# Attention by whole head-pair blocks instead of two-tile units, in a scheduled kernel of banded attention and two MLPs

## The chip, the cores and the metric

The kernel runs on one core of a Trainium2 chip. The metric is the device time of one execution in microseconds (us). A change counts as measured here when it moves the time by more than about 0.5%, 4.8 us.

## What is computed

Cut to what matters, with B, H, S, D = 4, 8, 576, 64, 512 model columns and 2048 hidden columns:

```python
scores = scale * np.matmul(q, k.transpose(0, 1, 3, 2))
mask = (rel >= 0) & (rel < 128)                     # each row sees itself and 127 rows before
scores = np.where(mask, scores + bias[None], -1e9)  # bias: a slope per head times -|rel|
attn = np.exp(scores - np.max(scores, axis=-1, keepdims=True))
attn = attn / (np.sum(attn, axis=-1, keepdims=True) + 1e-09)
x = np.matmul(attn, v)                              # laid out as 2304 rows x 512
h = x @ w_in                                        # first MLP, rational activation
g = (a0 + a1*h + a2*h*h + a3*h*h*h) / (1 + |b0|*|h| + |b1|*h*h + 1e-6)
x2 = g @ w_out
h2 = x2 @ w2_in                                     # second MLP, SiLU
out = (h2 / (1 + np.exp(-h2))) @ w2_out
```

## The kernel before, in words

The 2304 rows are 18 tiles of 128. The first MLP works on five blocks of 4, 4, 3, 4 and 3 tiles (`blk1`), the second on five of 4, 4, 4, 3 and 3 (`blk2`). A block takes 16 steps, one for each 128 of the 2048 hidden columns. A step makes h for its columns with 12 products (L726 to L728: four slices of the 512 model columns, each as high part by high part, high by low and low by high, since every fp32 operand is split into two fp32r halves), runs the activation on it and, two steps later (`lag`), adds 12 products into the block's accumulators (L805 to L807, in the second MLP L843 to L845). The first two blocks run interleaved (ten steps of block 0, ten of block 1, then six and six); then come blocks 2, 3, 4, and the second MLP's blocks 5 to 9.

The activation of the first MLP is six ScalarE (ACT) and six VectorE (DVE) instructions in a chain (L743 to L772). The last, `t3<-t1,h` at L772, frees the PSUM buffer of h; there are two of those (`hb`), so PE's h products wait for L772 of two steps before. Then g is split: `gh` is a cast of t3 (by ACT, DVE or POOL, as `OPT['gh']` allows), `gl` the remainder t3 - gh (POOL or DVE, `OPT['gl']`).

Weights are loaded as 64-bit numbers and put together by three instructions, one on ACT (L480) and two on DVE (`raw_w`, `raw_wo`: L482 and L484), then split into a high part (`hi`, L389 or L397) and a low part (`lo`, a TENSOR_TENSOR at L404 on DVE or L408 on POOL). For the second MLP `OPT['w2lo']` says who makes the low part. These 32 weights are prepared during block 4 and at the start of block 5.

Attention of a block runs ahead of its MLP steps, one head pair after another (four in a block). Before the change its unit is two tiles of one head pair (`unit`, 40 units). A unit has scores for both heads (`s`, L571), the other band half put in by a predicated copy (L580), mask and row maximum (L589), exp with row sums (L593), 1/sum (`l`, L604 and L605), normalization of `e` (L609 on POOL or L614 on ACT), transposes (`pt`, L625), the two masked halves (`ph`, L632 and L637), products with v (`av`, L662), a copy of `av` out of PSUM (`xr`, L389), and, once a head pair's block is complete, the split of `xr` into `xh` and `xl`, the operands of h.

The order on every engine is not written by hand. `plan_kernel` lists operations with a priority (in units of steps), one or several engines with a cost each, and what they read and write; `schedule` then simulates the engines with these costs, takes in turn the operation of least priority number among those that could start soonest (`look`, in ns), and chooses the engine. The instructions are issued in that order, and each engine executes its own queue strictly in order. The constants of `OPT` with decimals (`dS`, `dT`, `dA`: scores, transposes and products with v; `x2p`: loads of the second MLP's input; `pw`, `pwo`: weights; `wpro`, `lead`: pace of attention) are shifts of these priorities. `spin` products on an identity matrix fill PE's planned pauses before the first h.

Of the kernel before, what the change touches and what calls it, by code (L numbers as in the profile page):

```python
# [312 lines left out]
def plan_kernel(ctx, tc, qn, kn, vp, table, w1, wo1, a4, b2, w2, wo2, out):  # L313
# [231 lines left out]
    def unit(u, pS, pT, pA, w):  # L545
        gi, tiles = units[u]
        bi, hp = groups[gi]
        i0 = tiles[0] - blk_start[bi]
# [29 lines left out]
        if two:  # L578
            for hh in range(2):
                pl.op(pS + (0.05 + 0.01 * hh) * w, "dve", c_dve(nt_ * P), lambda hh=hh: nc.vector.copy_predicated(  # L580
                    T[S_[hh]][:, two, c1], tab[:, 4:5].bitcast(U32).broadcast_to([P, nt_, P]), T[S_[hh]][:, two, 0:P]),
                    reads=[("tab", 0)], writes=[S_[hh]])

        def mx(ti, hh):
            if ti == 0 and hh == 0:
                T[E_] = e_p.tile([P, 2, 2, P], F32, tag="e", name=f"e{u}")
                T[M_] = st_p.tile([P, 2, 2], F32, tag="m", name=f"m{u}")
                T[L_] = st_p.tile([P, 4, 1], F32, tag="l", name=f"l{u}")
            nc.vector.tensor_tensor_reduce(out=T[E_][:, ti, hh], in0=T[S_[hh]][:, ti, c1], in1=tabs[:, 2 * hp + hh, TABLE.get(tiles[ti], 0)],  # L589
                                           scale=-0.125, scalar=3.0e38, op0=ALU.add, op1=ALU.min, accum_out=T[M_][:, ti, hh:hh + 1])  # L590
# [30 lines left out]
        def tr():  # L621
            T[PT] = bank(PTT).tile([P, 2, 2, P], F32, tag=PTT, name=f"pt{u}")
            for ti in range(m):
                for hh in range(2):
                    nc.tensor.transpose(T[PT][:, ti, hh], T[E_][:, ti, hh], ident)  # L625
# [413 lines left out]
```

## Time and profile before

| what | value |
|---|---|
| median of 3 runs | 961.26 us (960.0 to 964.73) |
| profiled execution | 960.95 us, span of its instructions 959.2 us |
| PE (matmul) busy | 923.7 us, 96% of the span |
| DVE busy | 534.1 us, 56% |
| ACT busy | 550.9 us, 57% |
| POOL busy | 297.6 us, 31% |
| PE waits put down to DVE at L772 | 22.2 us in 26 waits |

The share of an engine over the whole span says little here, since the first 556 us (attention and first MLP) and the rest (second MLP) have different limits. The profile is therefore read by stretches. "fp32" matmuls appear as two records each, and matmul records overlap, so PE's pace is read from start to start.

### The profile page before, as it was taken

The numbers are of one execution on the slowest core, as the hardware profiler recorded it, in microseconds if no ns is written. First come the engines' busy times: TensorE is split into PE (matmuls) and PEld (weight loads), VectorE is DVE, ScalarE is ACT, GpSimd is POOL, SyncE is SP. The second block draws the span as 40 slices with busy tenths as digits, with TensorE's granted clock in tenths as the row PEclk, the third lists the DMA queues.
The fourth block names the chain that finished last, engine by engine and source line by source line (L and its number), as shares of the span: only waits on it lengthen the run. The fifth ranks groups of instructions, "written<-read, shape, count | busy, mean of one in ns | idle before, by whom it ended". The sixth has DMA issues, their size and how long they took to land.

```text
span 959.2 us, 13416 instructions
## 1 busy us (share of the span) xinstructions
PE 923.7 (96%) x4712; PEld 764.5 (80%) x4712; DVE 534.1 (56%) x1237; ACT 550.9 (57%) x1185; POOL 297.6 (31%) x277
## 2 busy tenths in 40 slices
PE   8879899999999999999988899999999999999998
PEld 6656677876678888777888888888888888999997
DVE  5889998789889888888899887200001000000000
ACT  6989898897676776766788675232223222222222
POOL 1134543454222122223222463342223223222221
PEclk9989999999999999999999999999999999999999
DMA  8365773476655334322475576111002000100000
GB/s 262 121 202 184 230 255 125 150 223 227 202 173 170 126 118 138 113 66 88 139 234 181 172 223 215 34 34 44 1 1 77 1 1 1 45 1 1 33 1 33
DMA packets 53842, 111.36 MB, mean 116 GB/s; under 512 B 4752, under 2 KB 24208, under 8 KB 53776
## 3 DMA queue, kind: packets, MB, share of 16 engines
q1 hardware_dynamic: 53776, 110.51, 35.7%
q8 instruction: 37, 0.61, 0.3%
q14 instruction: 29, 0.24, 0.1%
HBM read 90.57 MB, written 19.92 MB: 115 GB/s over the span
## 4 chain that ended last, share of the span: by engine, by line
PE 75%; DVE 11%; ACT 6%; DMA 5%; issue 2%; SPq 0%; POOL 0%; ACTq 0%; POOLq 0%; DVEq 0%
PE h L726 13%; PE h L728 12%; PE h L727 12%; PE acc L845 7%; PE acc L844 7%; PE acc L843 7%; PE acc L805 4%; PE acc L807 4%; PE acc L806 4%; PE s L571 3%; PE av L662 2%; DVE t L757 2%; DMA raw_wo<-in_wo 2%; ACT t L749 1%; DVE t L772 1%
## 5 line engine op out<-in xcount | busy, mean ns | idle before, releaser
L408 POOL TENSOR_TENSOR gl<-t,gh 128x512 fp32r<-128x512 f32 (+1 forms) x151 | 183.8, 1217 | 471.8 <-ACT gh L389 338.4
L779 ACT ACTIVATE t<-h 128x512 f32<-128x512 f32 (+1 forms) x80 | 44.5, 556 | 243.7 <-PE h L728 243.3
L805 PE MATMUL acc<-gh,wo 128*128 128x512 f32 (+1 forms) x320 | 123.3, 385 | 1.4 <-DVE x L826 0.8
L807 PE MATMUL acc<-gl,wo 128*128 128x512 f32 (+1 forms) x320 | 118.4, 370 | 0.0
L726 PE MATMUL h<-x2h,w 128*128 128x512 f32 (+1 forms) x320 | 118.0, 369 | 0.4 <-DVE t L772 0.4
L806 PE MATMUL acc<-gh,wo 128*128 128x512 f32 (+1 forms) x320 | 118.0, 369 | 0.0
L728 PE MATMUL h<-x2h,w 128*128 128x512 f32 (+1 forms) x320 | 117.9, 368 | 0.0
L727 PE MATMUL h<-x2l,w 128*128 128x512 f32 (+1 forms) x320 | 117.7, 368 | 0.0
L845 PE MATMUL acc<-wo,gl 128*128 128x512 f32 x288 | 112.7, 391 | 0.0
L844 PE MATMUL acc<-wo,gh 128*128 128x512 f32 x288 | 112.6, 391 | 0.0
L843 PE MATMUL acc<-wo,gh 128*128 128x512 f32 x288 | 112.0, 389 | 0.0
L726 PE MATMUL h<-xh,ws 128*128 128x512 f32 (+1 forms) x256 | 97.3, 380 | 11.6 <-DVE t L772 11.4
L404 DVE TENSOR_TENSOR x2l<-x2r,x2h 128x512 fp32r<-128x512 f32 (+1 forms) x8 | 7.0, 892 | 179.5 <-ACT x2h L389 179.5
L728 PE MATMUL h<-xh,ws 128*128 128x512 f32 (+1 forms) x256 | 93.6, 366 | 0.0
L727 PE MATMUL h<-xl,ws 128*128 128x512 f32 (+1 forms) x256 | 93.5, 365 | 0.0
L389 ACT CAST gh<-t 128x512 fp32r<-128x512 f32 (+1 forms) x141 | 81.1, 576 | 18.7 <-DVE t L772 15.4
L805 PEld LDWEIGHTS acc<-gh,wo 128*128 128x128 f32 x320 | 60.3, 188 | 16.3 <-issue 6.9
L726 PEld LDWEIGHTS h<-xh,ws 128*128 128x128 f32 x256 | 48.3, 189 | 25.9 <-DVE t L772 18.7
L726 PEld LDWEIGHTS h<-x2h,w 128*128 128x128 f32 x320 | 60.1, 188 | 9.8 <-PE acc L807 0.7
L743 ACT ACTIVATE t<-h,ab 128x512 f32<-128x512 f32 (+1 forms) x80 | 51.3, 641 | 28.5 <-PE h L728 28.2
L727 PEld LDWEIGHTS h<-x2l,w 128*128 128x128 f32 x320 | 60.1, 188 | 8.8
L807 PEld LDWEIGHTS acc<-gl,wo 128*128 128x128 f32 x320 | 60.2, 188 | 8.5 <-POOL gl L408 0.5
(86 smaller groups left out, 1850.0 us busy)
## 6 DMA issues: line engine op xcount, KB each, us to landing
ws<-sc SPq DMA_DIRECT2D x64, 512.0 KB, 3.3
raw_w<-in_w SPq DMA_DIRECT2D x32, 512.0 KB, 4.5
raw_wo<-in_wo SPq DMA_DIRECT2D x32, 512.0 KB, 4.5
sc<-w SPq DMA_DIRECT2D x16, 512.0 KB, 4.9
out<-out SPq DMA_DIRECT2D x18, 256.0 KB, 2.0
kd<-in_kn SPq DMA_DIRECT2D x12, 256.0 KB, 3.6
qd<-in_qn SPq DMA_DIRECT2D x12, 256.0 KB, 4.1
vh<-in_vp SPq DMA_DIRECT2D x12, 256.0 KB, 4.2
```

Of the source, the lines that this page charges most:

```text
L389: nc.scalar.activation(out=o, in_=i, func=AF.Copy, scale=sc) if scale is not None else nc.scalar.copy(o, i)
L408: nc.gpsimd.tensor_tensor(out=o, in0=a, in1=b, op=op)
L726: nc.tensor.matmul(o, lhsT=T[W][:, 0, c], rhs=xh, start=kt == 0, stop=False)
L727: nc.tensor.matmul(o, lhsT=T[W][:, 0, c], rhs=xl, start=False, stop=False)
L728: nc.tensor.matmul(o, lhsT=T[W][:, 1, c], rhs=xh, start=False, stop=kt == KD - 1)
L743: nc.scalar.activation(out=t("t2"), in_=hp_(), func=AF.Abs, scale=ab[:, 1:2])
L805: nc.tensor.matmul(a, lhsT=T[WO][:, 0, c], rhs=T[G1][:, :n], start=first_f, stop=False)
L806: nc.tensor.matmul(a, lhsT=T[WO][:, 1, c], rhs=T[G1][:, :n], start=False, stop=False)
L807: nc.tensor.matmul(a, lhsT=T[WO][:, 0, c], rhs=T[G2][:, :n], start=False, stop=last_f)
L843: nc.tensor.matmul(T[A], lhsT=T[G1][:, c], rhs=T[WO][:, 0], start=f == 0, stop=False)
L844: nc.tensor.matmul(T[A], lhsT=T[G1][:, c], rhs=T[WO][:, 1], start=False, stop=False)
L845: nc.tensor.matmul(T[A], lhsT=T[G2][:, c], rhs=T[WO][:, 0], start=False, stop=f == KF - 1)
```

## The change

The unit of attention becomes a head pair's whole block of 3 or 4 tiles (`group`, 20 groups). Scores, predicated copies, maxima and exps still run in halves of two tiles; the 1/sum is one pair of instructions for the group; normalization and transposes run in halves into two PSUM banks, one for each head; the masked halves are made for each head over the whole block; the products with v are one accumulation over up to 512 columns; and `xh` and `xl` are made straight from that PSUM bank, without `xr`. The allowed engines change (`gl` and the weights' low parts only on POOL, `gh` also on POOL, evacuations only on ACT), buffers of `e` and `ph` go from 3 and 2 to 2 and 1 (of larger tiles), and the priority shifts get other values.

```diff
-    'xh2': 'pool|act|dve',
-    'xl2': 'dve',
-    'gh': 'act|dve',
-    'gl': 'pool|dve',
+    'gh': 'act|dve|pool',
+    'gl': 'pool',
-    'evac': 'act|dve',
+    'evac': 'act',
-    'w2lo': 'dve',
-    'gl2': 'pool|dve',
+    'w2lo': 'pool',
+    'gl2': 'pool',
-    'eb': 3,
-    'ptb': 2,
+    'eb': 2,
+    'ptb': 1,
-    'tabs': 'pool|act',
+    'tabs': 'pool',
-    'wpro': 1.368,
-    'dS': -1,
+    'wpro': 1.204,
+    'dS': -1.576,
-    'dA': 0.194,
-    'dm': 0.315,
-    'look': 47.996,
-    'pw': -0.776,
-    'pwo': -1.143,
-    'x2p': 0.086,
+    'dA': 0.106,
+    'dm': 0.284,
+    'look': 28.673,
+    'pw': -0.74,
+    'pwo': -0.969,
+    'x2p': 1.653,
-    'dg': 0.371,
-    'lead': 2.2,
+    'dg': 0.44,
+    'lead': 2.526,
-    'gh0': 'act|pool',
+    'gh0': 'act',
...
-    def unit(u, pS, pT, pA, w):
-        gi, tiles = units[u]
+    def group(gi, pS, pT, pA, w):
         bi, hp = groups[gi]
+        t0, n = blk_start[bi], BLK1[bi]
+        tiles = list(range(t0, t0 + n))
...
+        ST = ("acc0", "acc1") if bi == 0 and gi % 2 else ("atA", "atB")
+        PTT = ("acc2", "acc3") if bi == 0 else ("atA", "atB")
+        AVT = ST[0] if bi == 0 else "atA"
+        halves = [range(a, min(a + 2, n)) for a in range(0, n, 2)]
...
+        ls = lambda a=0, b=n: T[L_][:, 2 * a:2 * b]
+        pl.op(pS + 0.5 * w, "dve", 100, lambda: nc.vector.tensor_scalar(out=ls(), in0=ls(), scalar1=1e-9, scalar2=None, op0=ALU.add), reads=[L_], writes=[L_])
+        pl.op(pS + 0.505 * w, "dve", 120, lambda: nc.vector.reciprocal(ls(), ls()), reads=[L_], writes=[L_])
...
+                nc.vector.tensor_tensor(out=T[PH][:, hh, :n, 0], in0=T[PT[hh]][:, :n], in1=own_mask().broadcast_to([P, n, P]), op=ALU.mult)
...
-            pl.op(pA + 0.1 * w, do_copy(OPT["xhi"], m * P, xraw, psum=True), 0, None, reads=[AV], writes=[XR + (i0,)])
...
+        pl.op(pA + 0.1 * w, do_copy(OPT["xhi"], n * P, xh_all, psum=True), 0, None, reads=[AV], writes=[XH, XL + ("a",)])
+        pl.op(pA + 0.15 * w, "dve", c_dve(n * P), lambda: nc.vector.tensor_tensor(
+            out=T[XL][:, :n * P], in0=T[AV][:, :n * P], in1=T[XH][:, :n * P].bitcast(F32), op=ALU.subtract), reads=[AV, XH], writes=[XL])
```

Where instructions moved, at the places that the prediction speaks of. First DVE in block 4, around steps 70 and 71 (in `t1_70`, `h70` the number is the step's; `raw_w25` is second-MLP weight 5, `wo22` an output weight 2). Before:

```order
L757 SCALAR_TENSOR_TENSOR t1_70_5492<-t2_70_5484,ab_113,h70_5454 128x384
L770 SCALAR_TENSOR_TENSOR h69_5405<-t3_69_5440,na_112,h69_5405 128x384
L761 TENSOR_TENSOR t3_70_5490<-t3_70_5490,h70_5454 128x384
L772 SCALAR_TENSOR_TENSOR t3_69_5440<-t1_69_5445,h69_5405 128x384
L762 SCALAR_TENSOR_TENSOR t3_70_5490<-t3_70_5490,na_112,h70_5454 128x384
L393 CAST gh69_5514<-t3_69_5440 128x384
L484 SCALAR_TENSOR_TENSOR raw_wo22_5338<-raw_wo22_5338 128x512
L768 SCALAR_TENSOR_TENSOR t1_70_5492<-t1_70_5492,h70_5454 128x384
L770 SCALAR_TENSOR_TENSOR h70_5454<-t3_70_5490,na_112,h70_5454 128x384
L404 TENSOR_TENSOR wo22_5527<-raw_wo22_5338,wo22_5527 128x512
L772 SCALAR_TENSOR_TENSOR t3_70_5490<-t1_70_5492,h70_5454 128x384
```

With the change:

```order
L760 SCALAR_TENSOR_TENSOR t1_70_5266<-t2_70_5253,ab_113,h70_5221 128x384
L775 SCALAR_TENSOR_TENSOR t3_69_5205<-t1_69_5211,h69_5171 128x384
L764 TENSOR_TENSOR t3_70_5258<-t3_70_5258,h70_5221 128x384
L482 SCALAR_TENSOR_TENSOR raw_w25_5158<-raw_w25_5158 128x512
L765 SCALAR_TENSOR_TENSOR t3_70_5258<-t3_70_5258,na_112,h70_5221 128x384
L480 TENSOR_SCALAR raw_wo23_5218<-raw_wo23_5218 128x512
L771 SCALAR_TENSOR_TENSOR t1_70_5266<-t1_70_5266,h70_5221 128x384
L773 SCALAR_TENSOR_TENSOR h70_5221<-t3_70_5258,na_112,h70_5221 128x384
L760 SCALAR_TENSOR_TENSOR t1_71_5320<-t2_71_5306,ab_113,h71_5275 128x384
L775 SCALAR_TENSOR_TENSOR t3_70_5258<-t1_70_5266,h70_5221 128x384
```

The low part (`wo22`) and the cast `gh69` are gone from DVE's queue; the six chain instructions of a step and the two that put a weight together stay.

POOL over the same steps, before:

```order
L408 TENSOR_TENSOR gl69_5524<-t3_69_5440,gh69_5514 128x384
L408 TENSOR_TENSOR gl70_5558<-t3_70_5490,gh70_5551 128x384
L408 TENSOR_TENSOR gl71_5620<-t3_71_5538,gh71_5616 128x384
L408 TENSOR_TENSOR gl72_5675<-t3_72_5592,gh72_5671 128x384
L408 TENSOR_TENSOR gl73_5725<-t3_73_5647,gh73_5714 128x384
```

With the change:

```order
L406 TENSOR_TENSOR gl69_5286<-t3_69_5205,gh69_5282 128x384
L406 TENSOR_TENSOR w25_5295<-raw_w25_5158,w25_5295 128x512
L395 TENSOR_SCALAR gh70_5335<-t3_70_5258 128x384
L406 TENSOR_TENSOR gl70_5339<-t3_70_5258,gh70_5335 128x384
L406 TENSOR_TENSOR wo23_5348<-raw_wo23_5218,wo23_5348 128x512
L395 TENSOR_SCALAR gh71_5388<-t3_71_5311 128x384
L406 TENSOR_TENSOR gl71_5392<-t3_71_5311,gh71_5388 128x384
```

In place of one instruction a step POOL now has three: the cast, the remainder, and a weight's low part.

Last, PE where the second MLP begins (`h80` is its first step, `acc4` the last accumulation of the first MLP). Before, from the second slice of h80 on:

```order
L728 MATMUL h80_5989<-x2h0_1_5810,w20_5100 128x512
L726 MATMUL h80_5989<-x2h0_2_5869,w20_5100 128x512
L727 MATMUL h80_5989<-x2l0_2_5876,w20_5100 128x512
L728 MATMUL h80_5989<-x2h0_2_5869,w20_5100 128x512
L726 MATMUL h80_5989<-x2h0_3_5905,w20_5100 128x512
L727 MATMUL h80_5989<-x2l0_3_5917,w20_5100 128x512
L728 MATMUL h80_5989<-x2h0_3_5905,w20_5100 128x512
L805 MATMUL acc4_0_0_5268<-gh78_5996,wo114_2439 128x384
```

With the change:

```order
L731 MATMUL h80_5764<-x2h0_1_5663,w20_4819 128x512
L808 MATMUL acc4_0_0_5036<-gh78_5756,wo114_2371 128x384
L809 MATMUL acc4_0_0_5036<-gh78_5756,wo114_2371 128x384
L810 MATMUL acc4_0_0_5036<-gl78_5771,wo114_2371 128x384
L808 MATMUL acc4_0_1_5044<-gh78_5756,wo114_2371 128x384
L809 MATMUL acc4_0_1_5044<-gh78_5756,wo114_2371 128x384
L810 MATMUL acc4_0_1_5044<-gl78_5771,wo114_2371 128x384
L808 MATMUL acc4_0_2_5052<-gh78_5756,wo114_2371 128x384
L809 MATMUL acc4_0_2_5052<-gh78_5756,wo114_2371 128x384
L810 MATMUL acc4_0_2_5052<-gl78_5771,wo114_2371 128x384
L729 MATMUL h80_5764<-x2h0_2_5758,w20_4819 128x512
L730 MATMUL h80_5764<-x2l0_2_5777,w20_4819 128x512
```

Before, all 12 products of h80 stood ahead of `acc4` for step 78; now the second half of h80 stands behind nine of those twelve. The third and fourth slices of the second MLP's input (`x2h0_2`, `x2h0_3`) are loaded later than before (`x2p`), and the products that need them moved back with them.

## Rows read from the trace of the kernel before

**Rows 1.** The page's first lines: span, busy time of each engine.
```profile
span 959.2 us, 13416 instructions
PE 923.7 (96%) x4712; PEld 764.5 (80%) x4712; DVE 534.1 (56%) x1237; ACT 550.9 (57%) x1185; POOL 297.6 (31%) x277
```
**Rows 2.** Who waited for whom: total us, times, longest; PE's first, DVE's table.
```profile
PE h L726 <- DVE t L772: 22.2, 26, 3.6
...
DVE s L580 <- DMA tab<-in_table: 7.0, 1, 7.0
```
**Rows 3.** Busy time by stretch: length, PE, PEld, DVE, ACT, POOL, clock, DMA, GB/s.
```profile
46.00:72.00 26.00, 20.97 (x112) 15.46 (x111) 22.16 (x64) 21.02 (x59) 10.04 (x9) 0.87 0.65 211
...
96.00:120.00 24.00, 20.90 (x112) 15.70 (x110) 23.07 (x49) 20.16 (x45) 13.45 (x12) 1.00 0.72 231
120.00:144.00 24.00, 22.89 (x110) 17.12 (x109) 23.31 (x47) 22.03 (x44) 10.87 (x10) 1.00 0.76 256
473.00:556.00 83.00, 73.46 (x387) 68.38 (x387) 75.15 (x139) 64.43 (x119) 26.87 (x27) 0.98 0.62 201
556.00:600.00 44.00, 44.00 (x199) 36.61 (x198) 36.30 (x54) 26.87 (x45) 21.83 (x19) 1.00 0.70 226
```
**Rows 4.** Timeline of PE in block 4: start, us, engine, line; first and last h.
```profile
473.05 0.33 PE L726 MATMUL h<-xh,ws 128*128 128x384 f32 x1
...
514.88 0.33 PE L726 MATMUL h<-xh,ws 128*128 128x384 f32 x1
...
517.31 0.34 PE L807 MATMUL acc<-gl,wo 128*128 128x384 f32 x1
...
555.55 0.47 PE L726 MATMUL h<-x2h,w 128*128 128x512 f32 x1 [0.42 <-DVE t L772]
```
**Rows 5.** DVE's groups in 473 to 556 us: busy us, mean ns, idle before.
```profile
L404 DVE TENSOR_TENSOR w<-raw_w,w 128x512 fp32r<-128x512 f32 x8 | 5.5, 686 | 0.0
L484 DVE SCALAR_TENSOR_TENSOR raw_w<-raw_w 128x512 uint32<-128x512 uint32 x6 | 5.4, 895 | 0.1
L484 DVE SCALAR_TENSOR_TENSOR raw_wo<-raw_wo 128x512 uint32<-128x512 uint32 x6 | 4.8, 805 | 0.0
L404 DVE TENSOR_TENSOR wo<-raw_wo,wo 128x512 fp32r<-128x512 f32 x6 | 4.5, 758 | 0.3 <-ACT wo L389 0.3
L482 DVE TENSOR_SCALAR raw_wo<-raw_wo 128x512 uint32<-128x512 uint32 x6 | 3.1, 521 | 0.0
L482 DVE TENSOR_SCALAR raw_w<-raw_w 128x512 uint32<-128x512 uint32 x6 | 2.8, 470 | 0.0
```
**Rows 6.** POOL's groups over the whole span: low part of a weight, cast gh.
```profile
L408 POOL TENSOR_TENSOR w<-raw_w,w 128x512 fp32r<-128x512 f32 x16 | 21.6, 1352 | 29.6 <-ACT w L389 25.1 <-PE av L662 2.5 <-issue 2.1
L397 POOL TENSOR_SCALAR gh<-t 128x512 fp32r<-128x512 f32 x8 | 5.0, 621 | 9.0 <-DVE t L772 7.8 <-DVE raw_w L482 1.2
```
**Rows 7.** Weight assembly on DVE, min/median/max ns (tile view of raw_w, raw_wo).
```profile
L484 DVE SCALAR_TENSOR_TENSOR raw_w<-raw_w x32: 678/689/1784, 35.2 to 597.5; 128x512 uint32<-128x512 uint32 x32
L482 DVE TENSOR_SCALAR raw_wo<-raw_wo x32: 398/424/1514, 50.2 to 605.8; 128x512 uint32<-128x512 uint32 x32
```
**Rows 8.** Timeline at 47 us: one POOL and one DVE instruction that overlap.
```profile
47.01 1.31 POOL L408 TENSOR_TENSOR w<-raw_w,w 128x512 fp32r<-128x512 f32 x1 [0.30 <-ACT w L389]
...
47.63 1.24 DVE L484 SCALAR_TENSOR_TENSOR raw_w<-raw_w 128x512 uint32<-128x512 uint32 x1
```
**Rows 9.** DVE's 1/sum instructions in attention, whole span.
```profile
L604 DVE TENSOR_SCALAR l<-l 128x4 f32<-128x4 f32 x32 | 6.0, 188 | 2.3 <-ACT e L593 2.3
L605 DVE RECIPROCAL l<-l 128x4 f32<-128x4 f32 x32 | 5.5, 171 | 0.2
```
**Rows 10.** Timeline of ACT: second and eighth xr copy (head pairs 0 and 3 done).
```profile
22.25 0.35 ACT L389 COPY xr<-av 128x256 f32<-128x256 f32 x1
...
45.39 0.34 ACT L389 COPY xr<-av 128x256 f32<-128x256 f32 x1
```
**Rows 11.** DMA issues, median us from issue to landing, 256 KB each.
```profile
x2r<-x2d SPq DMA_DIRECT2D x12, 256.0 KB, 3.5
```

More of the change, by code (lines that the diff above doesn't have):

```diff
@@ L569, in s_mm @@
                 for hh in range(2):
                     r = slice(64 * hh, 64 * hh + 64)
-                    nc.tensor.matmul(T[S_[hh]][:, ti, k0[ti] * P:], lhsT=T[("qd", gi)][r, i0 + ti], rhs=T[("kd", gi)][r, i0 + ti + k0[ti]:i0 + ti + 2],
-                                     start=True, stop=True)
-        pl.op(pS, "pe", 120 + m * c_pe4(2 * P), s_mm, reads=[("kd", gi), ("qd", gi)], writes=list(S_))
-        c1 = slice(P, 2 * P)
[L578 to L590, printed above, removed]
@@ L592, in ex @@
-        def ex(ti, hh):
-            nc.scalar.activation(out=T[E_][:, ti, hh], in_=T[E_][:, ti, hh], func=AF.Exp, bias=T[M_][:, ti, hh:hh + 1], scale=-1.0,
-                                 accum_out=T[L_][:, 2 * ti + hh])
-        parts = [(ti, hh) for hh in range(2) for ti in range(m)]
-        for j, (ti, hh) in enumerate(parts):
-            pl.op(pS + (0.1 + 0.01 * j) * w, "dve", c_dve(P) + 8, lambda ti=ti, hh=hh: mx(ti, hh), reads=[S_[hh], ("tabs", 2 * hp + hh)],
-                  writes=[E_ + (ti, hh), M_ + (ti, hh)] + ([L_ + (9,)] if j == 0 else []))
@@ L600, in unit @@
-        for j, (ti, hh) in enumerate(parts):
-            pl.op(pS + (0.2 + 0.02 * j) * w, "act", c_act(P, False, 2) + 90, lambda ti=ti, hh=hh: ex(ti, hh), reads=[E_ + (ti, hh), M_ + (ti, hh)],
-                  writes=[E_ + (ti, hh), L_ + (ti, hh)])
-        ls = lambda: T[L_][:, :2 * m]
-        pl.op(pS + 0.4 * w, "dve", 90, lambda: nc.vector.tensor_scalar(out=ls(), in0=ls(), scalar1=1e-9, scalar2=None, op0=ALU.add), reads=[L_], writes=[L_])
-        pl.op(pS + 0.41 * w, "dve", 100, lambda: nc.vector.reciprocal(ls(), ls()), reads=[L_], writes=[L_])
@@ L619, in unit @@
-        PT, PH = (PTT, f"pt{u}"), ("ph", u)
[L621 to L625, printed above, removed]
-        pl.op(pT, "pe", 2 * m * 109, tr, reads=[E_, ("ident", 0)], writes=[PT])
-        def own():
-            T[PH] = pt_p.tile([P, 2, 2, 2, P], F32, tag="ph", name=f"ph{u}")
-            nc.vector.tensor_tensor(out=T[PH][:, :m, 0], in0=T[PT][:, :m], in1=own_mask().broadcast_to([P, m, 2, P]), op=ALU.mult)
@@ L664, in unit, with xh_all @@
-        pl.op(pA, "pe", 200 + (m + nt_) * 215, av, reads=[("vh", gi), PH], writes=[AV])
+                    nc.tensor.matmul(T[AV][r, cs_], lhsT=v[:, iv, r], rhs=rhs(hh), start=k == 0, stop=k == len(steps) - 1)
+        pl.op(pA, "pe", 200 + (n + sum(1 - k for k in k0)) * 215, av, reads=[("vh", gi), PH], writes=[AV])
         XH, XL = (f"xh{hp}", f"1_{bi}"), (f"xl{hp}", f"1_{bi}")
         xkey[(bi, hp)] = (XH, XL)
-        cs = slice(i0 * P, (i0 + m) * P)
-        def new_x():
+        def xh_all():
```

199 lines of the change are left out of this document (114 added, 85 removed).

## Prediction

> **What bounds the kernel now.** I first read the page's head [rows 1]: PE is busy for 923.7 of 959.2 us. So a change can win only what PE loses: some 35 us in which it stands idle, a little more where it restarts or runs at the lower clock, less what the start and the last store need. The list of waits says to whom PE loses it [rows 2]: of what a named instruction of this program ends, nearly all is one pair, the first h product of a step waiting for DVE's L772, 22.2 us in 26 waits. L772 frees the PSUM buffer of h. The reader should see that this is DVE being late, not PE.
>
> The table by stretch says where [rows 3]. From 46 to 144 us, where attention of the first two blocks and the first steps share the engines, DVE is busy 22.16 of 26, then 23.07 and 23.31 of 24 us. From 473 to 556 us, which is block 4, DVE is busy 75.15 of 83 us, 90.5%, and PE only 73.46. After 556 us PE has no gap at all, and nothing done to DVE or ACT there can help.
>
> Block 4 has no attention beside it, so its floor is plain. Between the products at 514.88 and 517.31 us [rows 4] lie 14 starts without a wait, 0.174 us each. A step has 24, so 4.17 us, and 16 steps 66.7 us. They took from 473.05 to 555.55 [rows 4], 82.5 us. Some 16 us are lost here, more than the 9.5 us of PE idle, since a part lies in restarts.
>
> **The change, part by part. DVE in block 4.** The order shows the low parts gone from DVE. In block 4 there were 14 of them, 5.5 + 4.5 = 10.0 us [rows 5]. Of 12 + 12 instructions that put weights together, 11 + 11 remain, one of about 0.85 and one of about 0.50 us less [rows 5]: 1.3 us. DVE's work falls from 75.15 to 63.9 us. At the same busy share of 90.5% the stage would take 70.6 us.
>
> But POOL takes the 14 low parts at 1.35 us (18.9 us) and 13 casts gh at no more than 0.62 us [rows 6] (8.1 us): from 26.87 us in 83 [rows 3], 32%, to 53.9 us in about 74, 73%. The two engines get in each other's way. A DVE instruction that began at 47.63 us, while POOL worked on a low part from 47.01 us, took 1.24 us [rows 8], where the median of its kind is 0.69; the worst took 1.78, and the simpler one goes from 0.42 to 1.51 [rows 7]. In block 4 these 24 instructions exceed their medians by 6 x (0.206 + 0.116 + 0.097 + 0.046) = 2.8 us [rows 5, 7]. If that grows with POOL's share, it becomes 2.8 x 73/32 = 6.4 us, 3.6 more. DVE then has 67.5 us, and the stage takes 67.5/0.905 = 74.6 us: **-8.4 us**. The ends: -12.4 us (no more waiting, 70.6 us; PE's 66.7 is not reached), and 0, if each of the 22 remaining instructions waits 0.51 us more, which brings DVE back to 75.15. I take the middle value because the excess is measured at 32% and only its growth is assumed.
>
> The Trainium skill, page "SBUF — State Buffer", section "SBUF: two separate sides", speaks against this part: DVE and GpSimd have one port pair in common, an exclusive lock held for the whole instruction, so the later one blocks. The row at 47.63 us agrees: it ended about one normal duration after POOL's. By that rule an instruction under POOL's work waits for its remainder, 73% x half of 1.35 = 0.49 us; with 22 of these, 10.8 instead of 6.4 us, the stage would take 79.5 and the kernel some 955 us.
>
> **POOL's own queue.** A step of block 4 now brings POOL a cast, a remainder and a low part, at most 0.62 + 1.35 + 1.35 = 3.3 of 4.6 us. What is queued behind a low part that waits for its weight is the next gh and gl, for which PE waits two steps later. That lead, about 9 us, is the cover; if it were gone, each wait would cost PE up to 1.35 us. At the start of the second MLP POOL has 13 low parts and 8 remainders in the first 8 steps, 21 x 1.35 = 28 us, with two smaller ones 31 of 44 us (now 21.83 of 44 [rows 3]). It fits. I set 0. ACT gives up casts gh and had 64.43 of 83 us: no cost either.
>
> **DVE in blocks 0 and 1.** 16 pairs of 1/sum instructions become 8. A pair is 0.188 + 0.171 = 0.36 us [rows 9], so 2.9 us go where DVE is busy up to 97% of the time. The masks and `xl` keep their columns, so nothing else is gained. Between 0 and -2.9: **-2 us**. In blocks 2 to 4's attention, 24 pairs become 12, 4.3 us in a stretch where PE loses less to DVE (22.2 less the 9.5 of idle in block 4 and the 9.2 in the three stretches before 144 us [rows 3] leaves some 4): between 0 and -4, **-1 us**.
>
> **Copies.** 40 `xr` copies go, 20 casts to `xh` from PSUM take twice the columns, and ACT does these instead of POOL and DVE: ACT's work hardly changes, 0.
>
> **PE's instructions.** Scores, transposes and products with v keep their columns; 224 product instructions with v become 176. 0, at best -1.
>
> **The prologue.** Head pairs 0 to 3 are done at 22.25 and 45.39 us (first and last) [rows 10], 7.7 us apart. They overlap, because a unit of the next pair starts while the last is under way. With whole groups the sums wait for all exps of a pair and the masks for all its transposes, which lengthens one pair's chain, but two PSUM pairs keep two groups in flight. Between -2 and +12 (the third rival); I take **0**.
>
> **Start of the second MLP.** The loads of its input move behind weight loads in SP's queue, and h80's second half moves behind nine products (9 x 0.174 = 1.6 us of shelter). A load lands 3.5 us after its issue [rows 11], then come a cast and a subtraction. Between 0 and +3: **+1 us**.
>
> **Sum.** -8.4 - 2 - 1 + 0 + 1 = -10.4 us. The profiled execution took 960.95 us (span 959.2), 0.3 under the median of 961.26. So **950.5 us**, and 943 to 956 if only the terms' sizes are wrong.
>
> **Rivals.** *All of DVE's lateness goes.* If the lighter DVE queue never makes PE wait, the whole 22.2 us of L772 go: 939 us. For it: nearly all named waits are on this one instruction. Against it: DVE keeps six instructions a step, and its work in block 4 is near PE's floor.
>
> *POOL hands the time back.* If each weight instruction on DVE waits 0.51 us more for POOL, block 4 keeps its 83 us, and -2 - 1 + 1 leave 959 us, no change that can be told. For it: waits of up to 1.1 us stand in the rows [rows 7]. Against it: the mean excess now is only 0.12 us.
>
> *The groups are too coarse (slower).* Place: the prologue and block 1. The first pair alone took from the table's landing, about 7 us (DVE idles 7.0 for it [rows 2]), to 22.6 us, 15.6 us; later ones 7.7. If half of the overlap is lost, a pair takes 11.7 us: three pairs of block 0 come 12 us later, and block 1's four, partly hidden behind steps, add about 6. With the other terms that is 960.95 - 10.4 + 18 = 969 us. It decides against the change from 10.4/18 of that loss on, when a pair takes about 10 us. For it: one buffer of `ph` instead of two. Against it: halves still run on their own up to the exps.
>
> That the change does not do what it says is excluded by the order: the low parts stand on POOL.
>
> **How the numbers follow.** Forecast 0.56 (943 to 956), all lateness 0.13 (936 to 943), POOL hands it back 0.20 (955 to 963), too coarse 0.11 (962 to 975). Faster by over 0.5% (below 956.5 us; 0.5% is about what a measurement of this kernel can tell from no change): 0.56 + 0.13 + 0.05 of the third case = 0.74. Same: 0.15 + 0.02 = 0.17. Slower: 0.09. The range 939 to 962 leaves out about half of the second case and the last one, 0.17.
>
> **What would show it.** Right: in the stretch of block 4 (473 us on, or where it then lies) DVE's busy time near 67 us, no low part on it, the stretch 71 to 78 us long, and PE's waits for the last chain instruction well under 22.2 us in all. Half wrong: the medians of the weight instructions unchanged but their means above 1.1 us. Wrong: block 4 as long as before, or the second MLP's first product at 556 us or later, with PE's waits ended by exps, normalization or transposes before 130 us.

## The result, and the profile after

The changed kernel takes 947.62 us (median of 4 runs, 946.98 to 950.36) against 961.81 us for the kernel before in the same series: a ratio of 0.9855, 95% interval 0.9823 to 0.9887, some 14 us faster. The forecast was 950.5 us in 939 to 962. Its profiled execution took 947.48 us. The head of its page, beside [rows 1]: the span is 14.2 us shorter, and PE's share of it a point higher.

```profile
span 945.0 us, 13200 instructions
PE 915.5 (97%) x4620; PEld 761.3 (81%) x4620; DVE 509.9 (54%) x1147; ACT 538.2 (57%) x1143; POOL 361.5 (38%) x339
```

The list of waits of PE, beside [rows 2]. L729 and L775 are the h product and the last chain instruction that were L726 and L772.

```profile
PE h L729 <- DVE t L775: 7.0, 17, 1.3
PE s L575 <- DVE xl L694: 6.2, 4, 2.5
...
PE av L682 <- DVE ph L654: 1.8, 4, 0.7
```

The wait that held the kernel fell from 22.2 to 7.0 us. A new one took second place: scores wait for `xl`, all four times before 65 us. `xl` now reads the PSUM bank of `av` itself, and the next head pair's scores need that bank.

The table by stretch, with the columns of [rows 3]. Block 4 now lies between 464.20 and 541.20 us (first h products of steps 64 and 80).

```profile
46.00:72.00 26.00, 20.26 (x109) 13.13 (x107) 21.95 (x75) 20.59 (x63) 6.15 (x6) 0.93 0.51 166
72.00:96.00 24.00, 24.00 (x140) 18.15 (x140) 22.90 (x62) 22.01 (x56) 10.86 (x9) 1.00 0.50 144
96.00:120.00 24.00, 22.59 (x117) 17.32 (x113) 22.29 (x38) 19.66 (x36) 12.12 (x10) 1.00 0.73 236
120.00:144.00 24.00, 22.29 (x100) 17.35 (x101) 23.32 (x50) 23.14 (x45) 10.01 (x8) 1.00 0.72 236
464.20:541.20 77.00, 71.69 (x385) 66.49 (x384) 68.85 (x124) 62.24 (x111) 51.05 (x51) 1.00 0.68 216
541.20:585.00 43.80, 43.65 (x198) 36.31 (x197) 36.84 (x36) 27.47 (x49) 38.45 (x30) 1.00 0.66 203
```

Block 4 lasts 77.0 instead of 82.5 us; DVE has 68.85 us of work in it, POOL 51.05. The granted clock over the stage rose from 0.98 to 1.00, which by estimate (2% of 82.5 us) is up to 1.6 of the 5.4 us. DVE is still as full as before from 72 to 144 us.

By stage, from the starts of the first h products: block 4 starts at 464.2 instead of 473.1 us, so **8.9 us were won ahead of it, 5.4 in it, and about none after it** (from its end to the start of block 6, step 96: 86.5 against 86.4 us). The forecast had -3, -8.4 and +1.

DVE's weight instructions in block 4 (groups of DVE by shape, columns as in [rows 5]):

```profile
L482 DVE SCALAR_TENSOR_TENSOR raw_w<-raw_w 128x512 uint32<-128x512 uint32 x7 | 5.6, 803 | 0.0
L482 DVE SCALAR_TENSOR_TENSOR raw_wo<-raw_wo 128x512 uint32<-128x512 uint32 x7 | 5.4, 773 | 0.0
L480 DVE TENSOR_SCALAR raw_w<-raw_w 128x512 uint32<-128x512 uint32 x7 | 4.3, 613 | 0.0
L480 DVE TENSOR_SCALAR raw_wo<-raw_wo 128x512 uint32<-128x512 uint32 x6 | 3.7, 621 | 0.2 <-DMA raw_wo<-in_wo 0.2
```

The same groups in the first 44 us of the second MLP, where POOL is busy for 38.45 of 43.8 us:

```profile
L482 DVE SCALAR_TENSOR_TENSOR raw_w<-raw_w 128x512 uint32<-128x512 uint32 x6 | 9.4, 1565 | 0.6
L482 DVE SCALAR_TENSOR_TENSOR raw_wo<-raw_wo 128x512 uint32<-128x512 uint32 x7 | 8.8, 1254 | 0.6 <-ACT raw_wo L478 0.2
L480 DVE TENSOR_SCALAR raw_w<-raw_w 128x512 uint32<-128x512 uint32 x6 | 7.2, 1195 | 2.6 <-DMA raw_w<-in_w 2.6
L480 DVE TENSOR_SCALAR raw_wo<-raw_wo 128x512 uint32<-128x512 uint32 x7 | 5.9, 843 | 2.5 <-DMA raw_wo<-in_wo 2.5
```

### The profile page after: what moved, and what is told of

Its sections match the earlier page's. It is cut to its first block, busy times and chain, and to the rows that moved or that the text cites. A ratio compares the mean times of both kernels' runs of the same rounds, so it can differ in the third digit from the quotient of the medians.

```text
span 945.0 us, 13200 instructions
## 1 busy us (share of the span) xinstructions
PE 915.5 (97%) x4620; PEld 761.3 (81%) x4620; DVE 509.9 (54%) x1147; ACT 538.2 (57%) x1143; POOL 361.5 (38%) x339
## 4 chain that ended last, share of the span: by engine, by line
PE 76%; DVE 11%; ACT 6%; DMA 4%; issue 1%; POOL 1%; SPq 0%; ACTq 0%; DVEq 0%; POOLq 0%
PE h L729 13%; PE h L730 12%; PE h L731 12%; PE acc L847 7%; PE acc L848 7%; PE acc L846 7%; PE acc L808 4%; PE acc L810 4%; PE acc L809 4%; PE s L575 3%; PE av L682 2%; DVE t L760 2%; ACT t L752 1%; DVE t L775 1%; ACT t L746 1%
## 5 line engine op out<-in xcount | busy, mean ns | idle before, releaser
L406 POOL TENSOR_TENSOR gl<-t,gh 128x512 fp32r<-128x512 f32 (+1 forms) x160 | 196.6, 1229 | 275.6 <-ACT gh L387 253.3
L402 DVE TENSOR_TENSOR x2l<-x2r,x2h 128x512 fp32r<-128x512 f32 (+1 forms) x10 | 11.0, 1115 | 202.9 <-ACT x2h L387 202.9
L729 PE MATMUL h<-x2h,w 128*128 128x512 f32 (+1 forms) x320 | 117.9, 368 | 0.2 <-DVE t L775 0.2
L395 POOL TENSOR_SCALAR gh<-t 128x512 fp32r<-128x512 f32 (+1 forms) x58 | 33.0, 569 | 188.1 <-DVE t L775 143.9
L729 PE MATMUL h<-xh,ws 128*128 128x512 f32 (+1 forms) x256 | 96.3, 376 | 5.0 <-DVE t L775 4.9
L746 ACT ACTIVATE t<-h,ab 128x512 f32<-128x512 f32 (+1 forms) x80 | 51.3, 641 | 33.4 <-PE h L731 32.6
L760 DVE SCALAR_TENSOR_TENSOR t<-t,ab,h 128x512 f32<-128x512 f32 (+1 forms) x80 | 55.3, 691 | 26.2 <-ACT t L752 25.1
L763 ACT ACTIVATE t<-t 128x512 f32<-128x512 f32 (+1 forms) x80 | 47.1, 589 | 37.6 <-DVE t L760 36.7
L729 PEld LDWEIGHTS h<-x2h,w 128*128 128x128 f32 x320 | 60.1, 188 | 9.3 <-DVE t L775 0.5
```

The costliest lines, as they stand in the source:

```text
L406: nc.gpsimd.tensor_tensor(out=o, in0=a, in1=b, op=op)
L729: nc.tensor.matmul(o, lhsT=T[W][:, 0, c], rhs=xh, start=kt == 0, stop=False)
L746: nc.scalar.activation(out=t("t2"), in_=hp_(), func=AF.Abs, scale=ab[:, 1:2])
L760: nc.vector.scalar_tensor_tensor(out=t("t1"), in0=t("t2"), scalar=ab[:, 0:1], in1=hp_(), op0=ALU.add, op1=ALU.mult)
```

## The experiments

Each edit also makes the planner order the work anew, so a difference holds the edit and what the new order does with it. The intervals reach 1 to 3 us to each side; 4 us between two rows is just clear of them. "Block 4 from" is the start of step 64, "long" the time to step 80, both from each run's trace (for `b_w2lo` from `b_w2lo_look`).

| kernel | ratio to before, 95% | us to before (ratio less 1, times 961) | block 4 from | long |
|---|---|---|---|---|
| before | 1 | 0 | 473.1 | 82.5 |
| after | 0.9855 (0.9823 to 0.9887) | -13.9 | 464.2 | 77.0 |
| `b_w2lo` | 0.9994 (0.9981 to 1.0007) | -0.6 | 472.3 | 82.9 |
| `a_w2lo` | 0.9898 (0.9878 to 0.9918) | -9.8 | 464.4 | 81.0 |
| `b_eng` | 0.9969 (0.9953 to 0.9985) | -3.0 | 474.4 | 79.6 |
| `a_eng` | 0.9946 (0.9928 to 0.9964) | -5.2 | 465.1 | 78.6 |
| `a_num` | 0.9951 (0.9933 to 0.9970) | -4.7 | 473.8 | 77.8 |
| `a_half` | 0.9898 (0.9879 to 0.9917) | -9.8 | 467.4 | 77.2 |
| `a_xr` | 0.9945 (0.9921 to 0.9969) | -5.3 | 471.4 | 79.4 |
| `a_raw` | 0.9872 (0.9849 to 0.9896) | -12.3 | 464.3 | 80.2 |
| `a_h4` | 0.9965 (0.9946 to 0.9984) | -3.4 | 464.6 | 80.5 |
| `b_h4` | 0.9961 (0.9943 to 0.9980) | -3.7 | 473.4 | 79.5 |
| `a_h4w` | 0.9847 (0.9827 to 0.9867) | -14.7 | 463.8 | 70.6 |

### The low parts alone, added and taken away

`b_w2lo` is the kernel before with one line of the change, `a_w2lo` the changed kernel without it.

```diff
-    'w2lo': 'dve',
+    'w2lo': 'pool',
```

> The kernel before with one change: the low parts of the second MLP's weights go to POOL. PE's order stays the same from end to end. Theory (block 4 was bound by DVE's queue, and the low parts on it cost what block 4 lost): block 4, from its first h product to the second MLP's first one, falls from 82.5 us to about 77, and nothing before it moves, so about 956 us in all. Rival (POOL hands the time back, since the weight instructions left on DVE wait for it): block 4 at 81 us or more, 960 us or more. Rival (the new places and groups did it, the engine does not matter): no change, 961 us.

> The changed kernel with the low parts of the second MLP's weights back on DVE. Theory: block 4 goes from 77.0 us back to about 82.5, all stages before it keep their lead, so about 953 us. Rival (the lighter POOL frees the weight instructions on DVE, which makes up for it): 950 us or less, with the mean of these instructions in block 4 near their median of 0.69 and 0.42 us.

Alone the line gains nothing; taken from the changed kernel it costs 4 us, all in block 4. `b_w2lo` was run once more for its trace:

> The kernel before with the low parts of the second MLP's weights on POOL, once more, for its trace. The times showed no gain (0.9994). Theory of the prediction (DVE's lighter work shortens block 4): the stage is 76 to 78 us and something after it gives the gain back. Theory after a_raw (DVE's work isn't the bound, the chain is): DVE's busy time in block 4 falls by some 9 us, and the stage stays at 80 us or more.

Its table by stretch for block 4, then its DVE groups there:

```profile
472.30:555.20 82.90, 73.18 (x386) 68.01 (x384) 73.59 (x130) 63.89 (x119) 46.35 (x45) 0.98 0.63 209
```

```profile
L484 DVE SCALAR_TENSOR_TENSOR raw_w<-raw_w 128x512 uint32<-128x512 uint32 x7 | 6.6, 937 | 0.0
...
L482 DVE TENSOR_SCALAR raw_wo<-raw_wo 128x512 uint32<-128x512 uint32 x7 | 4.7, 665 | 0.0
...
L404 DVE TENSOR_TENSOR x2l<-x2r,x2h 128x512 fp32r<-128x512 f32 x2 | 2.2, 1091 | 0.2 <-POOL x2h L397 0.2
L404 DVE TENSOR_TENSOR gl<-t,gh 128x384 fp32r<-128x384 f32 x1 | 1.1, 1083 | 0.0
```

My expectation of 9 us less DVE work was a miss: 14 low parts went (10.0 us), and DVE's time fell by 1. In their place stand four more weight instructions, longer ones (TENSOR_SCALAR on `raw_wo` 665 against 521 ns [rows 5]), a `gl` and an evacuation. The steps 64 to 75 took 58.2 against 59.5 us before, the last four 24.7 against 23.0. So with the line the middle of the stage was shorter and its end longer; that the engine lists of before, which let such work go to DVE, lost it there is likely, but not shown. This run can't tell DVE's work from its order.

### The engine lists

`b_eng` is before with the seven lists of the change, `a_eng` the changed kernel with those of before.

```diff
-    'gh': 'act|dve',
-    'gl': 'pool|dve',
-    'evac': 'act|dve',
-    'w2lo': 'dve',
-    'gl2': 'pool|dve',
-    'tabs': 'pool|act',
-    'gh0': 'act|pool',
+    'gh': 'act|dve|pool',
+    'gl': 'pool',
+    'evac': 'act',
+    'w2lo': 'pool',
+    'gl2': 'pool',
+    'tabs': 'pool',
+    'gh0': 'act',
```

> The kernel before (units of two tiles, its own places) with all seven lists of allowed engines of the changed one. Theory (DVE and ACT are relieved by the lists, 10 us of low parts and some 5 us of casts, remainders and copies of DVE, 20 us of ACT's casts): block 4 near 77 us, some 2 to 4 us won in blocks 0 to 3, about 953 us. Rival (the gain ahead of block 4 comes from the whole-block groups alone): 956 us, with block 4's first product at 473 us as before.

> The changed kernel (whole-block groups, its places) with all seven lists of allowed engines of the kernel before. Theory: block 4 back at about 82.5 us; the groups' fewer 1/sum instructions and copies keep 5 to 7 of the 8.9 us won ahead of block 4, about 955 us. Rival (the lists made the gain ahead of block 4 too): block 4's first product back near 473 us, 960 us or more.

The lists alone give 3 us, all in block 4. Groups and places without them give 5: in the trace of that kernel they hold most of the lead ahead of block 4 (465.1 us), win 3.9 us in it and lose 3 us after it (89.6 us from step 80 to 96). This trace is of an execution of 952.3 us, one of the quickest of eleven (median 956.1), so it shows more gain than the ratio does. The two together give 14, more than the sum of the parts.

### The groups and the places

`a_num` gives the changed kernel the ten numbers of before:

```diff
-    'wpro': 1.204,
-    'dS': -1.576,
+    'wpro': 1.368,
+    'dS': -1,
...
-    'x2p': 1.653,
+    'x2p': 0.086,
...
-    'lead': 2.526,
+    'lead': 2.2,
```

> The changed kernel with the ten priority numbers of the kernel before; whole head pairs and the new engine lists stay. Theory (the 8.9 us won ahead of block 4 come from the whole head pairs: fewer 1/sum instructions, no xr, no POOL casts of xh): block 4 still starts within 3 us of 464 and the kernel takes 947 to 952 us. Rival (they come from the places): block 4 starts near 470 to 473 as before, and the kernel takes 954 to 958 us.

The rival came true: block 4 starts at 473.8 us, and 9 us are gone. Half of it is lost by step 4, which starts at 88.1 instead of 83.4 us, the rest on the way; block 4 itself keeps its length. So whole head pairs with the new lists, in the old places, win only what block 4 wins. Which of the two wins it there, this run doesn't tell; by `a_w2lo` most of it is the low parts.

`a_half` makes 1/sum for each half of a group:

```diff
-        pl.op(pS + 0.5 * w, "dve", 100, lambda: nc.vector.tensor_scalar(out=ls(), in0=ls(), scalar1=1e-9, scalar2=None, op0=ALU.add), reads=[L_], writes=[L_])
-        pl.op(pS + 0.505 * w, "dve", 120, lambda: nc.vector.reciprocal(ls(), ls()), reads=[L_], writes=[L_])
+        for a, half in enumerate(halves):
+            lh = lambda half=half: ls(half[0], half[-1] + 1)
+            lk = [L_ + (i, hh) for i in half for hh in range(2)]
+            pl.op(pS + (0.5 + 0.1 * a) * w, "dve", 90, lambda lh=lh: nc.vector.tensor_scalar(out=lh(), in0=lh(), scalar1=1e-9, scalar2=None, op0=ALU.add), reads=lk, writes=lk)
+            pl.op(pS + (0.505 + 0.1 * a) * w, "dve", 100, lambda lh=lh: nc.vector.reciprocal(lh(), lh()), reads=lk, writes=lk)
```

> The changed kernel with the 1/sum pair made for each half of a group instead of once for the group: 20 pairs more on DVE, 36 to 38 of them against 20. Theory of the prediction (the pairs cost what they take where DVE is busy, 0.36 us each, 3 us in blocks 0 to 3): 949 to 951 us, block 4 starts 2 to 4 us later. Rival (a half's normalization can start earlier, and that is worth as much): no change, within 1 us of 947.6.

40 pairs ran, 20 more than in the changed kernel. Block 4 starts 3.2 us later, the time is 4 us longer: with the new order that goes with it, the pairs cost about what the forecast's two terms for them said (3 us).

`a_xr` restores the copy out of PSUM:

```diff
-        pl.op(pA + 0.1 * w, do_copy(OPT["xhi"], n * P, xh_all, psum=True), 0, None, reads=[AV], writes=[XH, XL + ("a",)])
+        pl.op(pA + 0.1 * w, do_copy(OPT["xhi"], n * P, xraw, psum=True), 0, None, reads=[AV], writes=[XR])
+        pl.op(pA + 0.12 * w, do_copy("pool|act|dve", n * P, xh_all), 0, None, reads=[XR], writes=[XH, XL + ("a",)])
...
-            out=T[XL][:, :n * P], in0=T[AV][:, :n * P], in1=T[XH][:, :n * P].bitcast(F32), op=ALU.subtract), reads=[AV, XH], writes=[XL])
+            out=T[XL][:, :n * P], in0=T[XR][:, :n * P], in1=T[XH][:, :n * P].bitcast(F32), op=ALU.subtract), reads=[XR, XH], writes=[XL])
```

> The changed kernel with the copy of the product with v out of PSUM restored: ACT copies it to xr, a cast on POOL, ACT or DVE makes xh, and xl is the remainder from xr. Theory (the straight split cost and gave nothing: ACT's work stays the same and POOL is idle there): within 2 us of 947.6. Rival (the straight split gave several us of the 8.9 ahead of block 4, since the cast of xh shares engines with the activation of steps 0 to 47): 951 to 956 us, with block 4 starting 4 us or more later than 464.

Again the rival: 8.6 us lost, 7.2 of them ahead of block 4, and 4.0 of these by step 4 (87.4 against 83.4 us). Two groups of DVE up to there, and the min/median/max of all 20 `xl`, show a part of the price. In `a_xr`:

```profile
L701 DVE TENSOR_TENSOR xl<-xr,xh 128x512 fp32r<-128x512 f32 x12 | 9.9, 824 | 3.5 <-POOL xh L395 3.4
...
L701 DVE TENSOR_TENSOR xl<-xr,xh 128x384 fp32r<-128x384 f32 x8 | 5.6, 703 | 2.1 <-POOL xh L395 2.1
...
L701 DVE TENSOR_TENSOR xl<-xr,xh x20: 548/686/1781, 24.8 to 460.1; 128x512 fp32r<-128x512 f32 x12, 128x384 fp32r<-128x384 f32 x8
```

and in the changed kernel:

```profile
L694 DVE TENSOR_TENSOR xl<-av,xh 128x512 fp32r<-128x512 f32 x12 | 8.2, 682 | 2.5 <-ACT xh L387 2.3
...
L694 DVE TENSOR_TENSOR xl<-av,xh 128x384 fp32r<-128x384 f32 x8 | 4.4, 551 | 0.2 <-ACT xh L387 0.2
...
L694 DVE TENSOR_TENSOR xl<-av,xh x20: 549/678/692, 23.2 to 452.5; 128x512 fp32r<-128x512 f32 x12, 128x384 fp32r<-128x384 f32 x8
```

From SBUF, `xl` takes 142 and 152 ns more on the mean, 12 x 0.142 + 8 x 0.152 = 2.9 us of DVE, and DVE stands 3.4 + 2.1 us for POOL's cast, against 2.3 + 0.2 us for ACT's. The medians are alike (686 and 678 ns); single instructions make the difference, up to 1781 ns from SBUF, and none over 692 from PSUM. PE's waits for the last chain instruction are 14.2 us there, twice the 7.0. The Trainium skill, page "SBUF — State Buffer", section "SBUF: two separate sides", names as holders of the shared port a DVE instruction with two SBUF inputs against a GpSimd instruction that reads SBUF; `xl` from PSUM has one, and these rows agree.

The three edits together would cost 20 us ahead of block 4, where the change won 8.9: each takes away what the others need, and their shares can't be added.

### What bounds block 4

`a_raw` takes the assembly of the second MLP's weights from DVE:

```diff
+            if name in ("w1", "wo1"):
-            pl.op(p - 0.5, "dve", c_dve2x(NR), lambda: nc.vector.tensor_scalar(
+                pl.op(p - 0.5, "dve", c_dve2x(NR), lambda: nc.vector.tensor_scalar(
...
-            pl.op(p - 0.3, "dve", c_dve(NR), lambda: nc.vector.scalar_tensor_tensor(
+                pl.op(p - 0.3, "dve", c_dve(NR), lambda: nc.vector.scalar_tensor_tensor(
```

> Leaves out the two DVE instructions that assemble each weight of the second MLP, so the output isn't the reference's. DVE loses some 27 instructions of 0.6 to 0.8 us (with what they wait for POOL) in block 4, 19 us of its 66.5. Theory (DVE still bounds block 4): the stage falls from 77.0 to 67 to 70 us and the kernel to 938 to 941 us. Rival (what is left of block 4's loss is PE's own or comes through POOL's gh and gl): the stage stays at 74 us or more, the kernel at 945 us or more.

Its table by stretch for the first eight steps and for the stage, then DVE's waits in the stage:

```profile
464.30:503.50 39.20, 36.03 (x193) 33.39 (x191) 26.63 (x49) 30.63 (x56) 24.95 (x27) 1.00 0.73 239
...
464.30:544.50 80.20, 72.31 (x386) 68.20 (x385) 53.79 (x98) 64.64 (x119) 56.40 (x59) 0.98 0.75 244
```

```profile
DVE t L770 <- ACT h L768: 15.2, 16, 1.8
DVE t L759 <- ACT t L751: 7.5, 7, 3.1
```

DVE lost 15 us of work, and the stage got longer. What DVE had as work it now has as waiting for ACT's links of the chain. So a stage that follows DVE's work at a fixed busy share falls. But the run isn't clean: ACT stood in it behind two instructions that wait for something outside the chain, and every link queued behind them stood too (waits of ACT in the stage):

```profile
ACT t L745 <- POOL x2l L406: 2.5, 1, 2.5
...
ACT x L387 <- DMA x2d<-x: 2.4, 1, 2.4
```

The changed kernel has neither wait in its block 4. Without these 4.9 us the stage would be some 75 us by estimate, still far from the 67 to 70 expected. That DVE's work costs a few us here isn't excluded. The other candidate is the length of the chain. The timeline of the changed kernel, around steps 72 to 74, shows it:

```profile
502.53 0.44 PE L729 MATMUL h<-xh,ws 128*128 128x384 f32 x1 [0.26 <-DVE t L775]
...
504.92 0.58 ACT L746 ACTIVATE t<-h,ab 128x384 f32<-128x384 f32 x1
...
511.35 0.55 DVE L775 SCALAR_TENSOR_TENSOR t<-t,h 128x384 f32<-128x384 f32 x1
511.95 0.44 PE L729 MATMUL h<-xh,ws 128*128 128x384 f32 x1 [0.26 <-DVE t L775]
```

Step 72 takes its PSUM buffer at 502.53, its products are done and its chain starts at 504.92, the chain ends at 511.35 + 0.55 = 511.90, and the buffer's next user, step 74, starts at 511.95. A buffer is held for 9.4 us, there are two, so a step takes 4.7 us, and 16 take 75.2. Nine steps in a row, 69 to 77, take 4.6 to 4.7 us each. PE's own time for a step is 4.17 us. This alone does not name the bound: as long as PE takes each buffer when it is released, a buffer is held for two steps, whatever sets the pace.

If the number of buffers is the bound, a third and a fourth must lift it. In block 4 attention's banks are free:

```diff
-        Hk = ("h", g)
+        Hk = (("h", "h", "atA", "atB")[g % 4] if blk == nb1 - 1 else "h", g)
+        hp_pool = att_ps if Hk[0][:2] == "at" else h_p
...
-                T[Hk] = h_p.tile([P, 512], F32, tag="h", name=f"h{g}")
+                T[Hk] = hp_pool.tile([P, 512], F32, tag=Hk[0], name=f"h{g}")
```

> The changed kernel with four PSUM buffers for h in block 4 instead of two: the two banks of attention, which is done by then, are added. Every engine's order is the same up to block 4. Theory after a_raw (block 4 is held by the length of one step's chain over ACT and DVE, which frees h, not by DVE's work): PE's waits for the last chain instruction go from block 4 (4.2 us in 12 waits now), with the restarts behind them; the stage falls from 77.0 to 68 to 72 us and the kernel to 939 to 943 us. Rival (the work tiles t1 to t3, of which there are two each, or DVE's 69 us of work hold it as well): the stage stays at 75 us or more, and the waits turn up at ACT's first instructions of the chain or at the products that take g; 946 us or more.

> The kernel before with four PSUM buffers for h in block 4 instead of two; nothing else, and the same order on every engine up to block 4. If the chain's length held block 4 before, the stage falls from 82.5 to 72 to 77 us and the kernel to 951 to 956 us, and most of what the change won in block 4 could have been had without moving work from DVE. Theory of the prediction (DVE's 75.15 us of work at 90.5% are the stage): 80 us or more, 958 us or more.

Both miss what was expected of them: the stages take 80.5 and 79.5 us, the kernels 958 us, `a_h4` 10 us more than the changed kernel and `b_h4` 4 us less than the kernel before. The cause is my edit: the planner counted the new tenants of these banks as attention (a condition in the edit that was to except them, not shown, never held), and the second MLP's weights, which take over attention's SBUF, came late. But until the lack of weights stops it, PE goes at its own pace: 4.2 us a step for eleven steps on end or more, in either kernel. The first eight steps of `a_h4`:

```profile
464.60:499.90 35.30, 34.91 (x193) 33.57 (x192) 25.81 (x48) 24.23 (x44) 11.65 (x15) 1.00 0.45 143
```

and of `b_h4`:

```profile
473.40:508.10 34.70, 34.70 (x193) 33.67 (x192) 27.98 (x52) 27.63 (x50) 7.40 (x8) 1.00 0.46 144
```

DVE has about as much work there as in `a_raw`, where the same steps took 39.2 us with two buffers. But POOL and ACT have less, since none of the second MLP's weights is prepared in these steps, and the chain is shorter. Step 72 of `b_h4`, its first product and its last chain instruction:

```profile
508.13 0.33 PE L727 MATMUL h<-xh,ws 128*128 128x384 f32 x1
...
515.18 0.55 DVE L773 SCALAR_TENSOR_TENSOR t<-t,h 128x384 f32<-128x384 f32 x1
```

The buffer is held for 7.6 us (8.1 in `a_h4`), 3.8 (4.1) a step with two buffers, less than PE's own 4.17: two would have done. So these two runs can't tell the buffers from the missing weights, and `a_h4w` has to. It mends the count, so that the weights are prepared on time (against the changed kernel, beside the lines above):

```diff
-    last_att = [o for k, l in pl.tile_ops.items() if k[0] in ("kd", "qd", "vh", "e", "ph", "m", "l", "atA", "atB", "tab", "tabs") for o in l]
+    last_att = [o for k, l in pl.tile_ops.items() if k[0] in ("kd", "qd", "vh", "e", "ph", "m", "l", "atA", "atB", "tab", "tabs") if k[0][:2] != "at" or isinstance(k[1], str) for o in l]
```

> As a_h4, four PSUM buffers for h in block 4, but with the preparation of the second MLP's weights where the changed kernel has it: in a_h4 it waited by mistake for the new tenants of attention's banks, and most of it fell behind block 4. Theory (the turn of the two h buffers, the length of one step's chain, holds block 4): the first eight steps take 34 to 36 us as in a_h4 instead of 38.3, now with DVE's full work; the stage 68 to 72 us; the start of the second MLP gives back 0 to 4 us, since the weights then have less time; the kernel 938 to 945 us. Rival (a_h4's quick first half came from the weights that were missing there): the first eight steps take 37.5 us or more, the stage 75 us or more, the kernel 946 us or more.

Its table by stretch, first half and whole of block 4 and the 22 us behind it, then ACT's timeline at 532 us:

```profile
463.80:498.30 34.50, 33.29 (x181) 31.45 (x180) 28.63 (x54) 26.93 (x49) 19.52 (x22) 1.00 0.69 228
...
463.80:534.40 70.60, 68.28 (x374) 64.50 (x373) 60.46 (x111) 54.47 (x100) 44.02 (x46) 1.00 0.65 215
534.40:556.50 22.10, 18.76 (x85) 14.96 (x84) 20.04 (x25) 19.26 (x36) 17.64 (x14) 1.00 0.66 198
```

```profile
531.65 0.57 ACT L770 ACTIVATE h<-t,lnb 128x384 f32<-128x384 f32 x1
534.22 0.58 ACT L747 ACTIVATE t<-h,ab 128x384 f32<-128x384 f32 x1 [1.99 <-POOL x2l L406]
```

By the starts of PE's products the theory seems to hold: the first eight steps take 34.5 us, and step 80 starts 70.6 us after step 64. But these stretches hold fewer products (374 records against 385 in the stage, 181 against 193 in its first half) and less of DVE's work (60.46 against 68.85 us), for with four buffers PE makes h further ahead of the chain. What has to be compared is when the chains end. Steps 76 and 79 in the changed kernel (72 stands above):

```profile
530.11 0.55 DVE L775 SCALAR_TENSOR_TENSOR t<-t,h 128x384 f32<-128x384 f32 x1
...
546.02 0.54 DVE L775 SCALAR_TENSOR_TENSOR t<-t,h 128x384 f32<-128x384 f32 x1
```

and in `a_h4w` the first product of step 72, then the ends of the chains of 72, 76 and 79:

```profile
498.32 0.33 PE L730 MATMUL h<-xh,ws 128*128 128x384 f32 x1
...
511.13 0.55 DVE L776 SCALAR_TENSOR_TENSOR t<-t,h 128x384 f32<-128x384 f32 x1
...
527.96 0.55 DVE L776 SCALAR_TENSOR_TENSOR t<-t,h 128x384 f32<-128x384 f32 x1
...
546.98 0.54 DVE L776 SCALAR_TENSOR_TENSOR t<-t,h 128x384 f32<-128x384 f32 x1
```

The chain of step 72 ends 0.2 us earlier than with two buffers, that of 76 2.1 us earlier, that of 79 1.0 us later. The buffer of step 72 is held for 13.4 us (498.32 to 511.68) instead of 9.4. So two more buffers let PE run ahead, and the chains hardly came sooner: the number of buffers was not shown to hold block 4, and the rival, that `a_h4` was quick because weights were missing, is the likelier one. PE then loses its lead. It stands for 3.3 of the next 22 us, step 83 starts at 556.5 against 557.1 us in the changed kernel, and the kernel takes 946.26 us, above the 938 to 945 expected, which the intervals can't tell from 947.62.

What is left as the bound is the pace of the chain itself, over ACT and DVE with the work on the weights between its links: in step 72 it takes 7.0 us from 504.92 on in the changed kernel, 5.8 us in `a_h4` and 5.3 us in `b_h4` (from 510.41), without that work. Which engine's part of that work it is, and how much is the order, stays open. The row at 534.22 us shows one more hold on the chain: its first instruction waits for `x2l` on POOL, since the loads of the second MLP's input (`x2r`) borrow the work tiles `t1` and `t2`, of which there are two each, from the chain. It is the wait of 2.5 us that `a_raw` has too. Lifting it was not tried.

## Why the prediction was right, and where it wasn't

**The total.** 950.5 us was 2.9 us too high, and the direction stands. But two terms were off in opposite directions, so the closeness is partly luck.

**DVE in block 4, -8.4: -5.4.** The direction was right, the size was not. No low part on DVE, 68.85 us of work (forecast 67.5), a stage of 77.0 us (74.6; "71 to 78" was given as right). That one line, the low parts on POOL, is worth 4 us of the stage, `a_w2lo` shows: 81.0 us without it. The -8.4 is counted from the row's 83 us; from the stage's own 82.5 it is -7.9. And PE's floor of 66.7 us was some 1.3 us too low: the first eight steps take 34.7 us without a gap in `b_h4`, not 8 x 4.17 = 33.4. The makeup of the work was off: 27 weight instructions ran in the stage, not 22, some 2.8 us more, and they waited less for POOL. Their excess over their medians (0.424, 0.425, 0.688, 0.692 us) is 7 x (0.115 + 0.081) + 7 x 0.189 + 6 x 0.196 = 3.9 us; I had put 6.4. The step that failed is "at the same busy share of 90.5%". It fits the changed kernel, 68.85 of 77.0 being 89.4%, but it is no law: the share was 67% in `a_raw`, where ACT's links were what DVE waited for. In place of the share, the runs show a chain over two engines: work on the weights between its links goes with a longer one, 7.0 us against 5.8 and 5.3 without, and a longer step. How much of that is DVE's stays open. Before, four of the ten steps 64 to 73 took 5.7 us and the last four 23.0 us in all; after, none of steps 65 to 77 took over 5.0 and the last four 19.8.

**The rule on the shared port that the prediction cites.** By it I had a stage of 79.5 us and a kernel of 955. In block 4, with POOL busy for 66% of the time, the mean excess was 3.9/27 = 0.14 us instead of 0.49. At the start of the second MLP it was 6 x (0.877 + 0.771) + 7 x (0.562 + 0.418) = 16.7 us in 26 instructions, 0.64 each: there the price is as the rule gives it (88% x half of 1.35 = 0.59), and PE doesn't feel it (43.65 us busy of 43.8). Why the two engines meet so seldom in block 4 was not tried.

**POOL's queue, 0.** POOL's 51.05 us came as forecast (53.9), and PE's waits for `gl` are 1.1 us in the stage. Right. At the start of the second MLP POOL had 38.45 us, not 31: its instructions were longer there (`gl` of 128x512 1.63 us on the mean, counted at 1.35). That cost PE nothing.

**DVE in blocks 0 to 3, -2 and -1.** `a_half` puts the 1/sum pairs at 3.2 us, the new order included: right as far as that goes.

**Copies, 0.** Wrong, and one of the terms that mattered ahead of block 4. I had counted ACT's work, which hardly changes, and not whom the removed cast held up: `xl` on DVE waits for it, and from SBUF it takes longer. `a_xr` gives 7 us ahead of block 4, the new planner order included; the rows of `xl` account for 6 us of DVE's time at most, and how they become PE's was not followed.

**The places.** I had no term for the new numbers by themselves; `a_num` shows that without them the lead ahead of block 4 is gone. Which of the ten does it stays open.

**Prologue, 0, and the slower rival.** Step 4 starts at 83.4 instead of 82.4 us. Groups of four tiles are not too coarse in these places; in the old ones step 4 comes 4.7 us later.

**Start of the second MLP, +1: +0.1.** Within its bounds.

**The other rivals.** "All lateness goes": 15.2 of the 22.2 us went, and 6.2 came back as the new wait of the scores, ahead of block 1's steps, where little depends on it (step 4 starts 1 us later). "POOL hands it back" is what `b_w2lo` does, though by the planner's other choices rather than by 0.51 us an instruction.
